# Float32 numerator, normalisation on GpSimd, and a keys-values product with exp(k) stationary, in a three-stage kernel

## The chip, the cores and the metric

The kernel runs on one core of one Trainium2 chip as a single launch. The metric is the time of one execution on the device, in microseconds; each version is run several times and the median is given. Before the change the median of 3 runs is 1889.26 us (1889.13 to 1890.09).

## What is computed

Three stages follow one another. The first is a linear attention with exponential features; its result is the input of a dense layer, whose result is the input of a routed one.

```python
def phi(x):
    proj = einsum('bhsd,df->bhsf', x, w_phi)              # 8 batches, 8 heads, 576 tokens, 64 -> 128
    proj = proj - max(abs(proj), axis=-1, keepdims=True)
    return concatenate([exp(proj), exp(-proj)], axis=-1)  # 256 features
q_p, k_p = phi(q), phi(k)
kv  = einsum('bhsf,bhsd->bhfd', k_p, v)
z   = sum(k_p, axis=2)
num = einsum('bhsf,bhfd->bhsd', q_p, kv)
den = einsum('bhsf,bhf->bhs', q_p, z) + 1e-06
x   = num / den                                           # -> 4608 tokens of 512
h   = x @ w_in;  x = (h * cos(h)) @ w_out                 # 512 -> 2048 -> 512
# then each token goes to one of 8 experts (argmax of its logits), 512 -> 1024 -> 512
```

## The kernel before, in words

The attention works through 16 items, each of two batches (`bb`) and two heads (`h`). An item's 576 tokens are cut into five groups of blocks, `PR`; a group has two blocks of 128 columns, the middle one has one, with the leftover 64 tokens of both batches. The routine `step(j,s)` writes ten steps per item: keys, values and queries of item j, and the products with kv of item j-1. Within a step TensorE's instructions are written first; the work of the other engines stands in the lists `now`, `nxt` and `nxt2` and is written in the same step, the next one, or the one after that. The framework's scheduler then orders each engine's instructions, and every engine runs its own in that order.

For each group, by engine:

- TensorE projects keys and queries, three float32r products each (lines 130 to 132), into banks `pj`. VectorE takes the largest absolute value (line 137) and subtracts it (line 138), which gives `t_k` and `t_q`.
- ScalarE takes both exponentials of `t_k` (lines 149, 150) into `ke`. TensorE multiplies v, extended by a column of ones, with `ke` (line 168): v's 65 columns are the stationary operand, 256 columns of `ke` stream. The operands are float32, and each product stands as two instruction pairs (a weight load and a matmul) in the trace.
- When a batch is through, ScalarE copies its sums out (line 171), TensorE transposes them in four pieces (line 180), and VectorE writes kv, and z repeated 64 times, as a high part (lines 185, 186) and a remainder (lines 187, 188), both float32r.
- TensorE transposes `t_q` (line 203), ScalarE takes both exponentials into `qe` (lines 213, 214). A high part `qh` is copied, by VectorE or in one of five groups by ScalarE (line 219), and GpSimd subtracts it to get the remainder `ql` (line 220).
- `num` (line 241) makes numerator and denominator of half a batch (`u`): six float32r products of 288 columns per head. ScalarE takes ln, negation and exp (lines 249 to 251). VectorE multiplies (line 254), GpSimd prepares a Newton step (line 255), and VectorE applies it (line 257). After an item's last half SyncE's queue writes the result `xo` to the device's memory (line 260).

The last 20 of the 170 attention steps share the engines with the dense layer's start. There `stage` fetches a chunk of the dense weights through SyncE's queue (lines 411, 413), `decode` turns float64 bits into two float32r parts (ScalarE lines 427 and 433, VectorE lines 428 to 431, GpSimd line 434), 32 times in all, and the dense layer's first products (line 463) begin; VectorE has two instructions for each of their activations (lines 478, 481).

Of the kernel before, what the change touches and what calls it, by code (L numbers as in the profile page):

```python
# [43 lines left out]
def attention(tc, ctx, cpool, S, ps, ident, q, k, v, w_phi, xt):  # L44
    """generator; writes xt [4,128,4608], columns in the order of `chunk`"""
# [107 lines left out]
    kvp={}; kvt={}; kvsb={}  # L153
    def kv(i,g):
        """accumulate (v|1)^T k_p"""
# [3 lines left out]
        for idx in range(2*n):  # L159
            h,cc=chunk(c0,idx//2,idx%2)  # L160
            parts=[(0,0,P)] if cc<4 else ([(1,0,P)] if cc>4 else [(0,0,64),(1,64,P)])
            for (bb,p0,p1) in parts:
# [5 lines left out]
                nc.tensor.matmul(o,vh[p0:p1,h,cc,:],e[p0:p1,idx*256:(idx+1)*256],start=first and h==0,stop=last,skip_group_check=True)  # L168
                if last and h==1:
                    kt=S("kvt",f"kvt_{i}_{bb}")[0:D+1,:]  # L170
                    now.append(lambda kt=kt,p=kvp[i,bb]: nc.scalar.copy(kt,p[0:D+1,:]))
                    kvt[i,bb]=kt

    def kvfin(i,bb):
        """kv|z with f on partitions, z repeated 64 times; head 0: [kv|z], head 1: [z|kv]"""
        if i<0: return
        kt=kvt.pop((i,bb))
        pt=ps.tile([P,512],F32,tag="tr",name=f"pkv_{i}_{bb}")
        for g in range(4):
            nc.tensor.transpose(pt[:,g*(D+1):(g+1)*(D+1)],kt[:,g*P:(g+1)*P],ident[0:D+1,0:D+1])  # L180
        hi,lo=(S(x,f"{x}_{i}_{bb}",F32R).rearrange("p (s g d) -> p s g d",s=2,d=D) for x in ("kvh","kvl"))
        pv=pt[:,:4*(D+1)].rearrange("p (h s d) -> p s h d",h=2,s=2)
        z=pv[:,:,:,D:D+1].to_broadcast([P,2,2,D])
        def vec():
# [1 line left out]
            nc.vector.tensor_copy(hi[:,:,1:3,:],z)
            nc.vector.tensor_tensor(lo[:,:,0::3,:],pv[:,:,:,0:D],f32(hi[:,:,0::3,:]),ALU.subtract)
            nc.vector.tensor_tensor(lo[:,:,1:3,:],z,f32(hi[:,:,1:3,:]),ALU.subtract)
# [4 lines left out]
    def qtile(i,bb):
        if (i,bb) not in qq:
            qq[i,bb]=(ap.tile([P,2,2,576],F32R,tag="qh",name=f"qh_{i}_{bb}",bufs=3),
                      ap.tile([P,2,2,576],F32R,tag="ql",name=f"ql_{i}_{bb}",bufs=3))
        return qq[i,bb]
    def qexp(i,g,tt):
        """transpose proj - max, exp, split"""
# [12 lines left out]
        def vec():  # L212
            nc.scalar.activation(e[:,:,0,:w],pv,AF.Exp,scale=1.0)
            nc.scalar.activation(e[:,:,1,:w],pv,AF.Exp,scale=-1.0)
        def vec2():
            for (bb,s0,s1,d0) in parts:
                qh,ql=qtile(i,bb)
                sl=slice(d0,d0+s1-s0)
                (nc.scalar.copy if g==3 else nc.vector.tensor_copy)(qh[:,:,:,sl].rearrange("p h s c -> p (h s) c"),e[:,:,:,s0:s1].rearrange("p h s c -> p (h s) c"))  # L219
                nc.gpsimd.tensor_tensor(ql[:,:,:,sl],e[:,:,:,s0:s1],f32(qh[:,:,:,sl]),ALU.subtract)  # L220
        now.append(vec); nxt.append(vec2)

    xos={}
    def num(i,bb,u):
# [8 lines left out]
        rr=ap.tile([P,288],F32,tag="rr",name=f"rr_{i}_{bb}_{u}")
        pns=[]
        for h in range(2):
            pn=ps.tile([P,512],F32,tag="nm",name=f"pn_{i}_{bb}_{u}_{h}")[:,0:288]
            nmm=0
            for s in range(2):
                w=slice(h*P,(h+1)*P)
                for (A,B) in ((hi,qh),(hi,ql),(lo,qh)):  # L240
                    nc.tensor.matmul(pn,A[:,s,w],B[:,h,s,su],start=nmm==0,stop=nmm==5)
# [4 lines left out]
        # 1/den: exp(-ln den), then a Newton step  # L246
        def vec():
            for pn,a,b in pns:
                nc.scalar.activation(rr[a,:],pn[b,:],AF.Ln,bias=eps[b,:],scale=1.0)
# [700 lines left out]
```

## Time and profile before

| quantity | value |
|---|---|
| median of 3 runs | 1889.26 us |
| span of the profiled execution, first to last instruction | 1886.5 us |
| busy share of the span, TensorE matmul / VectorE / ScalarE / GpSimd | 93% / 65% / 54% / 36% |
| issues of the 16 results `xo` (line 260), first and last | 62.9 us, 524.3 us |
| last VectorE instruction of the last `decode` (line 431) | 621.0 us |

The page gives no time of its own for the profiled execution besides its span; the median is 2.8 us above that, for what lies around the instructions. In the views a row names the source line, the engine, the operation, the tile written and the tiles read, and the shapes. PE is TensorE's matmuls, PEld its weight loads, DVE VectorE, ACT ScalarE, POOL GpSimd, SP SyncE. A matmul's recorded time includes the time until its result has arrived, so matmuls that follow closely overlap in the records; their pace is the distance from start to start.

### The profile page before, as it was taken

To read this page: it belongs to the slowest core of one execution; us is meant where nothing else is said; L and a number is where in the kernel's file an instruction comes from. 1 tells how busy PE (TensorE), PEld (TensorE's weight loads), DVE (VectorE), ACT (ScalarE), POOL (GpSimd) and SP (SyncE) were. 2 spreads that over 40 slices of the span, in tenths; PEclk is the share of its full clock that TensorE was granted. 3 is DMA by queue.
4 is the path that set the end of the run, shared out by engine and by line. 5 is a ranking of instruction groups with operands and counts; after the bars stand their busy time and mean duration, and the time that the engine had idled before them with its cause. 6 is when DMAs were issued, how large, how long until landed. Compare 5 with 4: busy or idle time off the path is not lost. (4 is left out here: it accounts for less than half of the span.)

```text
span 1886.5 us, 27617 instructions
## 1 busy us (share of the span) xinstructions
PE 1759.9 (93%) x9782; PEld 1470.0 (78%) x9782; DVE 1232.9 (65%) x2168; ACT 1016.7 (54%) x1862; POOL 686.4 (36%) x556
## 2 busy tenths in 40 slices
PE   7989889898778899999999999999988999999996
PEld 6777777776556688888888888888877999999975
DVE  7999999999899545453545454444466655555555
ACT  5787877877655333334343433343345555555555
POOL 3454444545555424243424343333222211111121
PEclk9999999999899899999999999999998999999998
DMA  6223232231343010101010101010136865767766
GB/s 170 73 80 94 61 99 72 81 90 55 108 142 122 0 46 1 45 1 46 1 45 1 45 0 45 1 45 3 36 124 249 294 224 201 257 226 226 224 221 223
DMA packets 143448, 192.27 MB, mean 102 GB/s; under 512 B 64831, under 2 KB 89535, under 8 KB 143298
## 3 DMA queue, kind: packets, MB, share of 16 engines
q1 hardware_dynamic: 135346, 168.82, 27.9%
q0 software_dynamic: 7952, 21.54, 3.4%
...
## 5 line engine op out<-in xcount | busy, mean ns | idle before, releaser
L463 PE MATMUL ph<-x,w 128*128 128x512 f32 x1728 | 435.6, 401 | 32.8 <-DVE fr L481 23.2
L463 PEld LDWEIGHTS ph<-x,w 128*128 128x128 f32 x1728 | 325.9, 192 | 113.7 <-DVE fr L481 29.1
L493 PE MATMUL acc<-gh,w 128*128 128x512 f32 x1152 | 358.6, 392 | 2.9 <-DVE gh L483 1.7
L484 POOL TENSOR_TENSOR gl<-fr,gh 128x512 fp32r<-128x512 f32 x144 | 190.1, 1321 | 364.4 <-DVE gh L483 296.0
L672 DVE TENSOR_TENSOR m<-raw,m 128x512 fp32r<-128x512 f32 x336 | 219.4, 693 | 134.9 <-ACT m L671 134.6
L493 PEld LDWEIGHTS acc<-gh,w 128*128 128x128 f32 x1152 | 217.9, 189 | 48.8 <-DVE gh L483 2.0
L220 POOL TENSOR_TENSOR ql<-qe,qh 128x1024 fp32r<-128x1024 f32 (+1 forms) x96 | 175.5, 1835 | 176.9 <-DVE qh L219 147.1
L671 ACT CAST m<-raw 128x512 fp32r<-128x512 f32 x336 | 195.7, 618 | 71.2 <-PE mh L712 31.4
L493 PE MATMUL acc<-gl,w 128*128 128x512 f32 x576 | 225.7, 392 | 3.3 <-POOL gl L484 3.3
L476 ACT ACTIVATE n<-ph 128x512 int32<-128x512 f32 x144 | 85.6, 595 | 255.1 <-PE ph L463 252.1
L478 DVE SCALAR_TENSOR_TENSOR fr<-ph,n 128x512 f32<-128x512 f32 x144 | 99.2, 689 | 181.8 <-ACT n L476 177.9
L712 PEld LDWEIGHTS mh<-xT,m 128*128 128x128 f32 x1728 | 210.8, 192 | 2.4 <-DVE hl L715 0.5
L712 PE MATMUL mh<-xT,m 128*128 128x256 f32 x1728 | 211.4, 283 | 0.2 <-DVE hl L715 0.2
L481 DVE SCALAR_TENSOR_TENSOR fr<-fr,ph 128x512 f32<-128x512 f32 x144 | 98.7, 686 | 159.0 <-ACT fr L480 159.0
L724 PE MATMUL po<-m,hh 128*128 128x512 f32 x576 | 181.6, 396 | 0.0
L479 ACT ACTIVATE fr<-fr 128x512 f32<-128x512 f32 x144 | 91.1, 632 | 145.1 <-DVE fr L478 143.8
L168 PE MATMUL kv<-ke,v 128*65 128x256 f32 (+1 forms) x640 | 148.9, 383 | 1.1 <-ACT ke L150 0.9
...
L493 PEld LDWEIGHTS acc<-gl,w 128*128 128x128 f32 x576 | 109.1, 189 | 27.2 <-POOL gl L484 4.4
L724 PEld LDWEIGHTS po<-m,hh 128*128 128x128 f32 x576 | 106.3, 190 | 20.4
L724 PE MATMUL po<-m,hl 128*128 128x512 f32 x288 | 113.1, 393 | 0.0
L168 PEld LDWEIGHTS kv<-ke,v 128*65 128x65 f32 (+1 forms) x640 | 74.6, 137 | 29.6 <-issue 3.4
(212 smaller groups left out, 3178.6 us busy)
## 6 DMA issues: line engine op xcount, KB each, us to landing
raw<-in_moe_w_dram SPq DMA_DIRECT2D x179, 512.0 KB, 6.4
...
```

The costliest lines, as they stand in the source:

```text
L168: nc.tensor.matmul(o,vh[p0:p1,h,cc,:],e[p0:p1,idx*256:(idx+1)*256],start=first and h==0,stop=last,skip_group_check=True)
L220: nc.gpsimd.tensor_tensor(ql[:,:,:,sl],e[:,:,:,s0:s1],f32(qh[:,:,:,sl]),ALU.subtract)
L463: nc.tensor.matmul(ph,A[:,ws],xhl[u,d][k],start=n[0]==0,stop=n[0]==11); n[0]+=1
L478: nc.vector.scalar_tensor_tensor(g,ph,INV2PI,n,op0=ALU.mult,op1=ALU.subtract)
L479: nc.scalar.activation(g,g,AF.Sin,scale=math.pi)
L481: nc.vector.scalar_tensor_tensor(g,g,-0.5,ph,op0=ALU.add,op1=ALU.mult)
L484: nc.gpsimd.tensor_tensor(gl,g,f32(gh),ALU.subtract)
L493: nc.tensor.matmul(accs[u][d],A[:,ws],B,start=(f==0 and k==0),stop=(f==NF-1 and k==2))
L671: nc.scalar.copy(h,a)
L672: nc.vector.tensor_tensor(l,a,f32(h),ALU.subtract)
L712: nc.tensor.matmul(ph[:,f2*T:(f2+1)*T],A[:,ws],B[d//2][:,xs],start=n==0,stop=n==11); n+=1
L724: nc.tensor.matmul(po[c],A[:,ws],B,start=(f==0 and j==0),stop=(f==NF2-1 and j==2))
```

## The change

Four things change in the attention; nothing changes behind it.

- kv: 128 columns of `ke` are stationary now and the 65 columns of v with ones stream. The sums come out with features on partitions, so the copy (line 171) and the transposes (line 180) go; VectorE copies kv and z from the bank into one float32 tile `kvz`.
- `qexp` writes the exponentials into one float32 tile `qx`, in place of `qe`, `qh` and `ql`.
- `num` has two float32 products per head and half, in place of six float32r ones.
- Per half, ScalarE writes the negated denominator and VectorE copies the numerator to `xo`. Per batch, ScalarE makes one ln and one exp over 576 columns, and GpSimd makes four instructions over 576 columns: the Newton step and the multiplication into `xo`.

```diff
                 if first and h==0:
                     kvp[i,bb]=ps.tile([P,512],F32,tag="kv",name=f"kv_{i}_{bb}")
-                o=kvp[i,bb][0:D+1,h*256:(h+1)*256]
-                nc.tensor.matmul(o,vh[p0:p1,h,cc,:],e[p0:p1,idx*256:(idx+1)*256],start=first and h==0,stop=last,skip_group_check=True)
-                if last and h==1:
-                    kt=S("kvt",f"kvt_{i}_{bb}")[0:D+1,:]
-                    now.append(lambda kt=kt,p=kvp[i,bb]: nc.scalar.copy(kt,p[0:D+1,:]))
-                    kvt[i,bb]=kt
+                for s in range(2):
+                    o=kvp[i,bb][:,(2*h+s)*66:(2*h+s)*66+D+1]
+                    nc.tensor.matmul(o,e[p0:p1,idx*256+s*F:idx*256+(s+1)*F],vh[p0:p1,h,cc,:],start=first and h==0 and s==0,stop=last,skip_group_check=True)
...
     def kvfin(i,bb):
...
-        for g in range(4):
-            nc.tensor.transpose(pt[:,g*(D+1):(g+1)*(D+1)],kt[:,g*P:(g+1)*P],ident[0:D+1,0:D+1])
...
         def vec():
-            nc.vector.tensor_copy(hi[:,:,0::3,:],pv[:,:,:,0:D])
-            nc.vector.tensor_copy(hi[:,:,1:3,:],z)
-            nc.vector.tensor_tensor(lo[:,:,0::3,:],pv[:,:,:,0:D],f32(hi[:,:,0::3,:]),ALU.subtract)
-            nc.vector.tensor_tensor(lo[:,:,1:3,:],z,f32(hi[:,:,1:3,:]),ALU.subtract)
+            nc.vector.tensor_copy(kz[:,:,0::3,:],pv[:,:,:,0:D])
+            nc.vector.tensor_copy(kz[:,:,1:3,:],z)
...
     def qexp(i,g,tt):
...
         def vec():
-            nc.scalar.activation(e[:,:,0,:w],pv,AF.Exp,scale=1.0)
-            nc.scalar.activation(e[:,:,1,:w],pv,AF.Exp,scale=-1.0)
-        def vec2():
             for (bb,s0,s1,d0) in parts:
-                qh,ql=qtile(i,bb)
-                sl=slice(d0,d0+s1-s0)
-                (nc.scalar.copy if g==3 else nc.vector.tensor_copy)(qh[:,:,:,sl].rearrange("p h s c -> p (h s) c"),e[:,:,:,s0:s1].rearrange("p h s c -> p (h s) c"))
-                nc.gpsimd.tensor_tensor(ql[:,:,:,sl],e[:,:,:,s0:s1],f32(qh[:,:,:,sl]),ALU.subtract)
-        now.append(vec); nxt.append(vec2)
+                qx=qtile(i,bb)
+                for k,sign in ((0,1.0),(1,-1.0)):
+                    nc.scalar.activation(qx[:,:,k,d0:d0+s1-s0],pv[:,:,s0:s1],AF.Exp,scale=sign)
+        now.append(vec)
...
     def num(i,bb,u):
...
             for s in range(2):
-                w=slice(h*P,(h+1)*P)
-                for (A,B) in ((hi,qh),(hi,ql),(lo,qh)):
-                    nc.tensor.matmul(pn,A[:,s,w],B[:,h,s,su],start=nmm==0,stop=nmm==5)
-                    nmm+=1
+                nc.tensor.matmul(pn,kz[:,s,h*P:(h+1)*P],qx[:,h,s,su],start=s==0,stop=s==1)
...
         def vec():
             for pn,a,b in pns:
-                nc.scalar.activation(rr[a,:],pn[b,:],AF.Ln,bias=eps[b,:],scale=1.0)
-                nc.scalar.activation(dn[a,:],pn[b,:],AF.Identity,bias=neps[b,:],scale=-1.0)
+                nc.scalar.activation(dn[a,su],pn[b,:],AF.Identity,bias=neps[b,:],scale=-1.0)
+                nc.vector.tensor_copy(xo[a,sl],pn[a,:])
+        now.append(vec)
+        if u==0: return
...
+        def inv():
+            nc.scalar.activation(rr,dn,AF.Ln,scale=-1.0)
             nc.scalar.activation(rr,rr,AF.Exp,scale=-1.0)
-        def vec2():
-            for pn,a,b in pns:
-                nc.vector.tensor_tensor(xo[a,sl],pn[a,:],rr[a,:],ALU.mult)
+        def mul():
             nc.gpsimd.tensor_tensor(dn,dn,rr,ALU.mult)
-        def vec3():
-            nc.vector.scalar_tensor_tensor(xo[:,sl],dn,2.0,xo[:,sl],op0=ALU.add,op1=ALU.mult)
-            if (bb,u)==(1,1):
+            nc.gpsimd.tensor_scalar(dn,dn,2.0,None,op0=ALU.add)
+            nc.gpsimd.tensor_tensor(dn,dn,rr,ALU.mult)
+            nc.gpsimd.tensor_tensor(xs,xs,dn,ALU.mult)
+            if bb==1:
                 bp,hp=items[i]
                 nc.sync.dma_start(xt[hp,:,bp*1152:(bp+1)*1152],xo)
-        now.append(vec); nxt.append(vec2); nxt2.append(vec3)
+        nxt.append(inv); nxt2.append(mul)
```

The scheduler's order at three places follows, before and after. Names carry the group, batch, half or head; the last number of a name tells buffers apart; "x4" is four such instructions in a row.

On TensorE, in the middle of the attention, the end of the second half's numerator of batch 0 (`pn_0_1_1`: batch, half, head) before the change:

```order
L241 MATMUL pn_0_1_1_3295<-qh_0_2858,kvh_0_3144 128x288
L241 MATMUL pn_0_1_1_3295<-ql_0_2859,kvh_0_3144 128x288
L241 MATMUL pn_0_1_1_3295<-qh_0_2858,kvl_0_3145 128x288
L180 MATMUL pkv_1_3302<-ident,kvt_1_3257 128x65 x4
L168 MATMUL kv_0_3330<-ke_0_3243,v_2780 65x256 x2
L203 MATMUL ptt_2_3309<-ident,t_q_2_3273 128x128 x4
```

The same place on TensorE after the change, the whole half with both heads:

```order
L223 MATMUL pn_0_1_0_2831<-qx_0_2469,kvz_0_2703 128x288 x2
L223 MATMUL pn_0_1_1_2834<-qx_0_2469,kvz_0_2703 128x288 x2
L168 MATMUL kv_0_2855<-v_2398,ke_0_2792 128x65 x4
L193 MATMUL ptt_2_2839<-ident,t_q_2_2824 128x128 x4
L168 MATMUL kv_0_2855<-v_2398,ke_0_2792 128x65 x4
```

The half has four products in place of twelve, the transposes of kv are gone, and a group's kv has eight products of 65 columns in place of four of 256.

On VectorE, the same stretch of an item before the change (`t_q_2` is what the transposes `ptt_2` read):

```order
L257 SCALAR_TENSOR_TENSOR xo_3218<-dn_0_0_3219,xo_3218 128x288
L138 TENSOR_TENSOR t_q_2_3273<-pj_q_2_3266,m_q_2_3283 128x512
L185 CAST kvh_1_3307<-pkv_1_3302 128x2x2x64
L186 CAST kvh_1_3307<-pkv_1_3302 128x2x128
L187 TENSOR_TENSOR kvl_1_3308<-pkv_1_3302,kvh_1_3307 128x2x2x64
L188 TENSOR_TENSOR kvl_1_3308<-pkv_1_3302,kvh_1_3307 128x2x128
L254 TENSOR_TENSOR xo_3218<-pn_0_1_0_3288,rr_0_1_3287 64x288
L254 TENSOR_TENSOR xo_3218<-pn_0_1_1_3295,rr_0_1_3287 64x288
L219 CAST qh_0_3241<-qe_2_3314 128x4x256
L137 TENSOR_REDUCE m_k_4_3357<-pj_k_4_3335 128x2
```

And on VectorE after the change:

```order
L178 COPY kvz_1_2838<-kv_1_2665 128x2x2x64
L179 COPY kvz_1_2838<-kv_1_2665 128x2x128
L136 TENSOR_REDUCE m_k_2_2825<-pj_k_2_2809 128x4
L136 TENSOR_REDUCE m_q_2_2828<-pj_q_2_2817 128x4
L137 TENSOR_TENSOR t_k_2_2816<-pj_k_2_2809,m_k_2_2825 128x512
L137 TENSOR_TENSOR t_q_2_2824<-pj_q_2_2817,m_q_2_2828 128x512
L230 COPY xo_2778<-pn_0_1_0_2831 64x288
L230 COPY xo_2778<-pn_0_1_1_2834 64x288
L136 TENSOR_REDUCE m_k_4_2883<-pj_k_4_2864 128x2
```

Nothing stands between the subtractions `t_k_2` and `t_q_2` and the reductions ahead of them; the copies to `xo` read banks alone and wait for no `rr`.

On SyncE's queue, where the attention ends, before the change (`st_0`, `st_1` are chunks of w_in and w_out, `xr` the dense layer's next input):

```order
L411 DMA st_0_6367<-in_moe_w_in_dram 128x4x256
L413 DMA st_1_6427<-in_moe_w_out_dram 128x1024
L260 DMA xt<-xo_6234 128x1152
L413 DMA st_1_6498<-in_moe_w_out_dram 128x1024
L443 DMA xr_0_7072<-xt 128x512
```

And after the change:

```order
L397 DMA st_0_5409<-in_moe_w_in_dram 128x4x256
L399 DMA st_1_5461<-in_moe_w_out_dram 128x1024
L246 DMA xt<-xo_5306 128x1152
L399 DMA st_1_5518<-in_moe_w_out_dram 128x1024
L429 DMA xr_0_6094<-xt 128x512
```

The order of the queue is the same; the write of `xo` follows GpSimd's multiplication now, where it followed VectorE's line 257.

More of the change, by code (lines that the diff above doesn't have):

```diff
@@ L59, in attention @@
     nc.scalar.preload_act_table_set("natural_log_exp_and_others")
-    eps=cpool.tile([P,1],F32,name="eps"); nc.vector.memset(eps,1e-6)
     neps=cpool.tile([P,1],F32,name="neps"); nc.vector.memset(neps,-1e-6)
@@ L151, in kexp @@
         es[i,g]=e
-    kvp={}; kvt={}; kvsb={}
+    kvp={}; kvsb={}
     def kv(i,g):
@@ L166, in kv @@
                     kvp[i,bb]=ps.tile([P,512],F32,tag="kv",name=f"kv_{i}_{bb}")
-                o=kvp[i,bb][0:D+1,h*256:(h+1)*256]
-                nc.tensor.matmul(o,vh[p0:p1,h,cc,:],e[p0:p1,idx*256:(idx+1)*256],start=first and h==0,stop=last,skip_group_check=True)
-                if last and h==1:
-                    kt=S("kvt",f"kvt_{i}_{bb}")[0:D+1,:]
-                    now.append(lambda kt=kt,p=kvp[i,bb]: nc.scalar.copy(kt,p[0:D+1,:]))
-                    kvt[i,bb]=kt
+                for s in range(2):
+                    o=kvp[i,bb][:,(2*h+s)*66:(2*h+s)*66+D+1]
+                    nc.tensor.matmul(o,e[p0:p1,idx*256+s*F:idx*256+(s+1)*F],vh[p0:p1,h,cc,:],start=first and h==0 and s==0,stop=last,skip_group_check=True)
     def kvfin(i,bb):
         if i<0: return
-        kt=kvt.pop((i,bb))
-        pt=ps.tile([P,512],F32,tag="tr",name=f"pkv_{i}_{bb}")
-        for g in range(4):
-            nc.tensor.transpose(pt[:,g*(D+1):(g+1)*(D+1)],kt[:,g*P:(g+1)*P],ident[0:D+1,0:D+1])
-        hi,lo=(S(x,f"{x}_{i}_{bb}",F32R).rearrange("p (s g d) -> p s g d",s=2,d=D) for x in ("kvh","kvl"))
-        pv=pt[:,:4*(D+1)].rearrange("p (h s d) -> p s h d",h=2,s=2)
+        pt=kvp.pop((i,bb))
+        kz=S("kvh",f"kvz_{i}_{bb}").rearrange("p (s g d) -> p s g d",s=2,d=D)
+        pv=pt[:,:4*66].rearrange("p (h s d) -> p s h d",h=2,s=2)
         z=pv[:,:,:,D:D+1].to_broadcast([P,2,2,D])
         def vec():
-            nc.vector.tensor_copy(hi[:,:,0::3,:],pv[:,:,:,0:D])
-            nc.vector.tensor_copy(hi[:,:,1:3,:],z)
-            nc.vector.tensor_tensor(lo[:,:,0::3,:],pv[:,:,:,0:D],f32(hi[:,:,0::3,:]),ALU.subtract)
-            nc.vector.tensor_tensor(lo[:,:,1:3,:],z,f32(hi[:,:,1:3,:]),ALU.subtract)
+            nc.vector.tensor_copy(kz[:,:,0::3,:],pv[:,:,:,0:D])
+            nc.vector.tensor_copy(kz[:,:,1:3,:],z)
         now.append(vec)
-        kvsb[i,bb]=(hi.rearrange("p s g d -> p s (g d)"),lo.rearrange("p s g d -> p s (g d)"))
+        kvsb[i,bb]=kz.rearrange("p s g d -> p s (g d)")
     qq={}
@@ L194, in qtile @@
         if (i,bb) not in qq:
-            qq[i,bb]=(ap.tile([P,2,2,576],F32R,tag="qh",name=f"qh_{i}_{bb}",bufs=3),
-                      ap.tile([P,2,2,576],F32R,tag="ql",name=f"ql_{i}_{bb}",bufs=3))
+            qq[i,bb]=ap.tile([P,2,2,576],F32,tag="qx",name=f"qx_{i}_{bb}",bufs=3)
         return qq[i,bb]
@@ L226, in num @@
         if i not in xos: xos[i]=ap.tile([P,9*P],F32,tag="xo",name=f"xo_{i}")
-        xo=xos[i]
-        hi,lo=kvsb[i,bb]
-        qh,ql=qtile(i,bb)
+        if u==0: dns[i,bb]=ap.tile([P,576],F32,tag="dn",name=f"dn_{i}_{bb}")
+        xo=xos[i]; dn=dns[i,bb]
+        kz=kvsb[i,bb]
+        qx=qtile(i,bb)
         sl=slice(bb*576+u*288,bb*576+(u+1)*288)
         su=slice(u*288,(u+1)*288)
-        dn=ap.tile([P,288],F32,tag="dn",name=f"dn_{i}_{bb}_{u}")
-        rr=ap.tile([P,288],F32,tag="rr",name=f"rr_{i}_{bb}_{u}")
         pns=[]
```

6 lines of the change are left out of this document (3 added, 3 removed).

## The prediction

> **What bounds the kernel now.** I read the page first, for where each engine is full. Its slices are 47 us each.
>
> ```profile
> span 1886.5 us, 27617 instructions
> ...
> PE   7989889898778899999999999999988999999996
> ...
> DVE  7999999999899545453545454444466655555555
> ```
>
> The attention fills the first eleven slices, and there VectorE is at nine tenths or more while TensorE has eights and sevens. From slice 14 on TensorE is full and VectorE half idle. The busy times by stage:
>
> ```profile
> core 0: us, PE busy (x) PEld busy (x) DVE busy (x) ACT busy (x) POOL busy (x), PEclk, DMA share, GB/s
> 100.00:454.00 354.00, 318.97 (x2233) 264.22 (x2232) 325.30 (x613) 279.79 (x590) 170.62 (x132) 1.00 0.28 80
> 454.00:525.00 71.00, 50.38 (x248) 39.86 (x248) 65.47 (x105) 51.36 (x91) 37.30 (x28) 0.88 0.25 83
> 525.00:621.00 96.00, 73.55 (x280) 55.24 (x280) 95.45 (x131) 48.46 (x84) 55.71 (x37) 0.91 0.39 127
> 640.00:700.00 60.00, 60.00 (x288) 48.78 (x288) 24.71 (x53) 22.77 (x37) 18.12 (x15) 1.00 0.11 36
> ```
>
> The groups of instructions from 100 to 454 us, VectorE's that the change touches:
>
> ```profile
> L257 DVE SCALAR_TENSOR_TENSOR xo<-dn,xo 128x288 f32<-128x288 f32 x48 | 54.0, 1126 | 0.0
> L254 DVE TENSOR_TENSOR xo<-pn,rr 64x288 f32<-64x288 f32 x97 | 44.0, 454 | 19.2 <-ACT rr L251 17.7
> L219 DVE CAST qh<-qe 128x1024 fp32r<-128x1024 f32 x36 | 24.8, 688 | 0.8
> L186 DVE CAST kvh<-pkv 128x256 fp32r<-128x256 f32 x24 | 9.8, 407 | 0.0
> L188 DVE TENSOR_TENSOR kvl<-pkv,kvh 128x256 fp32r<-128x256 f32 x24 | 9.8, 407 | 0.0
> L187 DVE TENSOR_TENSOR kvl<-pkv,kvh 128x256 fp32r<-128x256 f32 x24 | 9.8, 407 | 0.0
> L219 DVE CAST qh<-qe 128x256 fp32r<-128x256 f32 x24 | 5.8, 285 | 0.0
> ```
>
> Line 257 runs four times per item, so its 48 runs are 12 items in 354 us: 29.5 us per item. Of these VectorE is busy 27.1 (325.30/12) and idle mostly for `rr`; TensorE is busy 26.6 (318.97/12). From 454 to 621 us VectorE is at 92%, then 99%: decoding, the last items and the dense layer's start share it. After 640 us TensorE decides, in a part that the change leaves alone. So VectorE sets both the items' pace and the length of the passage, with TensorE close behind in the items; the question is what TensorE's new products cost. Its waits among the same groups:
>
> ```profile
> L203 PE MATMUL ptt<-ident,t_q 128*128 128x128 f32 x216 | 34.4, 277 | 26.8 <-DVE t_q L138 19.6 <-DVE kT_lo L119 7.3
> L241 PE MATMUL pn<-qh,kvh 128*128 128x288 f32 x192 | 60.4, 316 | 5.2 <-DVE kvh L186 2.9 <-DVE xo L254 2.3
> ```
>
> 32.0 us in 12 items, 2.7 per item, all for VectorE.
>
> **TensorE's products, per item.** Their pace is read from starts in the timeline, at a place without waits:
>
> ```profile
> 302.04 0.30 PE L241 MATMUL pn<-ql,kvh 128*128 128x288 f32 x1
> 302.17 0.29 PE L241 MATMUL pn<-qh,kvl 128*128 128x288 f32 x1
> 302.30 1.46 PE L168 MATMUL kv<-ke,v 128*65 128x256 f32 x6
> ...
> 304.07 0.28 PE L131 MATMUL pj_k<-wph_hi,kT_lo 128*128 128x256 f32 x1
> 304.18 0.28 PE L132 MATMUL pj_k<-wph_lo,kT_hi 128*128 128x256 f32 x1
> 304.30 0.60 PE L203 MATMUL ptt<-ident,t_q 128*128 128x128 f32 x4
> ```
>
> And, later, the transposes of kv, then the weight loads that belong to the six matmuls at 302.30:
>
> ```profile
> 308.35 0.41 PE L180 MATMUL pkv<-ident,kvt 65*128 65x65 f32 x4
> ```
>
> ```profile
> 302.18 1.13 PEld L168 LDWEIGHTS kv<-ke,v 128*65 128x65 f32 x6
> ```
>
> One float32r matmul of 288 columns takes 0.13 us, one of 256 takes 0.115, one float32 pass of 256 columns (1.46-0.38)/5 = 0.216 (0.38 being the record of one), a transpose of 128 columns (0.60-0.27)/3 = 0.11, one of kv's (0.41-0.22)/3 = 0.062. Per item there are 20 kv products with two passes, 48 numerator products, 54 projections, 36 transposes and 8 of kv: 40 x 0.216 + 48 x 0.13 + 54 x 0.115 + 36 x 0.11 + 8 x 0.062 = 8.6 + 6.2 + 6.2 + 4.0 + 0.5 = 25.5 us. With the waits of 2.7 that is 28.2; the last 1.3 us go to weight loads and pipeline ends around each wait.
>
> After it, the numerator has 16 float32 products, so 32 passes of 288 columns: 0.216 x 288/256 = 0.243 each, 7.8 us (+1.6). kv has 40 products, 80 passes, each a load of 128 columns and a stream of 65. The stream is short, 0.216 x 65/256 = 0.055 us, so the load sets the pace, and no row shows a true float32 load of 128 columns outside transposes. From below, kv's transposes load 128 columns in 0.062; from above stands a load's whole record, 0.19:
>
> ```profile
> L241 PEld LDWEIGHTS pn<-ql,kvh 128*128 128x128 f32 x192 | 36.2, 188 | 0.0
> L168 PEld LDWEIGHTS kv<-ke,v 128*65 128x65 f32 x384 | 49.9, 137 | 17.0
> ```
>
> I take 0.115, the projections' pace, in which a load of 128 columns fits: 63 more columns cost 51 ns of record whether the small load is float32 or the large one float32r, so the type does not seem to matter. That is 80 x 0.115 = 9.2 us (+0.6; ends 5.0 and 15.2). The transposes go (-0.5). TensorE: 25.5 + 1.6 + 0.6 - 0.5 = 27.2 us.
>
> This needs a load to run beside the previous matmul. The six loads start at 302.18 and spread over 1.13 us, while the six matmuls start at 302.30 and follow at 0.216, the pace of their streams alone; so they do. The Trainium skill, "TensorE: Matmul & The Clock Gate", Part 3, "The mechanism", says that a weight load overlaps matmuls in flight only when it goes to another row group; these all use the same rows, so this trace disagrees. By that rule the load, about P/1.2 or 107 ns by the same page's "LDWEIGHTS", would be added to the stream, and kv would take an estimated 13 us.
>
> **The other engines, per item.** VectorE loses lines 254 (44.0/12 = 3.7 us), 257 (4.5), 219 (30.6/12 = 2.5), 187 and 188 (1.6), 12.3 in all, and gains 8 copies of 64x288 from banks, between line 186's 0.41 for 256 and line 254's 0.45: 3.5 us. 27.1 - 8.8 = 18.3 us. ScalarE and GpSimd:
>
> ```profile
> L220 POOL TENSOR_TENSOR ql<-qe,qh 128x1024 fp32r<-128x1024 f32 x48 | 114.1, 2378 | 116.3 <-DVE qh L219 94.5 <-ACT qh L219 21.7
> L249 ACT ACTIVATE rr<-pn,eps 64x288 f32<-64x288 f32 x96 | 47.7, 497 | 12.0 <-PE pn L241 10.2
> L255 POOL TENSOR_TENSOR dn<-dn,rr 128x288 f32<-128x288 f32 x49 | 39.4, 803 | 55.4 <-ACT qT_hi L118 28.1 <-ACT rr L251 27.3
> L251 ACT ACTIVATE rr<-rr 128x288 f32<-128x288 f32 x48 | 21.1, 440 | 0.9
> L171 ACT COPY kvt<-kv 65x512 f32<-65x512 f32 x24 | 13.9, 581 | 0.0
> L219 ACT CAST qh<-qe 128x1024 fp32r<-128x1024 f32 x12 | 12.6, 1046 | 0.4
> ```
>
> ScalarE loses 95.3/12 = 7.9 us and gains four runs over 576 columns at 0.68 (between 0.44 for 288 and 1.05 for 1024) and two small exponentials: 23.3 to some 18.5. GpSimd loses lines 220 and 255, over 12.8 us (153.5/12), and gains eight runs over 576 columns; by line 255's 0.80 for 288 they take 1.6 each, 13 us. A scalar addition on GpSimd has no row; between 0.8 and 3 us it leaves GpSimd at 11 to 16 of 28 us, so it is covered, and would decide only at ten times that.
>
> New waits: the copies of `kvz` hold a kv bank until VectorE has read it, but two banks alternate, and the next use of one is almost an item later. GpSimd's four runs follow ScalarE's exp in a chain of about 6 us; behind it on GpSimd stands only the next batch's chain, and `xo` has two buffers.
>
> With VectorE at 18 and ScalarE at 19 of some 28 us, TensorE becomes the bound. In the scheduled order, after the last product of `pj_q` TensorE has a numerator (8 passes, 1.9 us) and half of a group's kv (0.9) before `ptt` needs `t_q`, against 0.3 of pipeline and three VectorE runs of 0.7 (2.4 us): covered by 0.4 us. I add 0.6 us for ends and short waits, 27.8 us per item. From the end of the first slice, in which inputs are still awaited, to 454 us there are (454 - 47)/29.5 = 14 items: 14 x 1.7 = 24 us. The ends are 27.2 (32 us) and 29.0, with nearly all waits still there (7 us).
>
> **The passage, 454 to 621 us.** VectorE's removed groups there (458 to 525 us):
>
> ```profile
> L257 DVE SCALAR_TENSOR_TENSOR xo<-dn,xo 128x288 f32<-128x288 f32 x8 | 9.4, 1174 | 0.1
> ...
> L254 DVE TENSOR_TENSOR xo<-pn,rr 64x288 f32<-64x288 f32 x14 | 6.3, 451 | 2.2 <-ACT rr L251 2.0
> ```
>
> With the last items' runs of lines 187, 188 and 219 (three of each, by the rows above 0.41, 0.41 and up to 0.69, 4.5 us) 20 us go, and 14 copies at 0.44 come (6.2). Records overlap a little; I count 12 us, all on the bound. Against it, the last write of `xo` now waits for GpSimd's chain, which stands between the dense layer's own subtractions there, and the chunk of w_out behind it on SyncE's queue lands later; a decode that waits for that chunk holds all of VectorE. GpSimd needs some 8 us more than line 257 did, and I find about as much VectorE work ahead of that decode: 2 us lost, between 0 and 9. Net 10 us, between 3 and 16.
>
> **Sum.** 24 + 10 = 34 us of the profiled 1886.5, so a span of 1852.5; with the 2.8 us between span and median, 1855 us.
>
> **The rivals.** *Slower, as weight loads are not hidden:* a pass of kv costs a load plus its stream, 0.115 + 0.055 = 0.17 us. kv takes 13.6 us, TensorE 31.6 + 0.6 = 32.2, 2.7 more than now; 14 x 2.7 - 10 = +28, 1917 us (0.19 gives 1939). It decides from 0.145 us per pass on, where item and passage cancel. For it: a short stream leaves less to hide a load behind than any float32 product shows. Against: the loads at 302.18. The overlap rule of the Trainium skill, on the page named above, ends here too, at an estimated 1908.
>
> *TensorE bound with its old waits:* queues in order keep 2 us of waits per item, though for other engines: 29.0 per item, 7 + 10 us, 1872. For it: ScalarE and VectorE stay two thirds full, and `ptt` has only 0.4 us of cover. Against: all 2.7 us of now are for an engine that loses a third of its work.
>
> *Much faster:* float32 loads go at the transposes' 0.062, TensorE needs 23.0, and with 2 us of waits items take 25: 14 x 4.5 + 10 = 73 us, 1816. Against: the 65-column loads of line 168 fit the slower pace.
>
> **How the numbers follow.** I give the forecast 0.64, old waits 0.20, unhidden loads 0.10, fast loads 0.06. A measurement of this kernel tells 0.2%, 3.8 us, from no change. Faster is 0.64 + 0.06 and old waits but for the 0.03 in which the passage gives its gain back too: 0.87; same 0.03; slower 0.10. Range: from 32 + 16 = 48 us (1841) less some for rounding, 1838, to 7 + 3 = 10 us (1879), taken as 1880; this leaves out the unhidden and the fast loads.
>
> **What would show it.** Right: issues of `xo` 27.8 us apart; kv passes at 0.115 us, numerator passes at 0.243; VectorE near two thirds busy in the items and TensorE's waits for `t_q` below 1 us per item; VectorE still full in the passage, which ends some 34 us earlier. Wrong: kv passes over 0.145, items over 29 us with waits of TensorE for ScalarE or VectorE, or VectorE waiting in the passage for a decode's input behind the last `xo` write.

## The result and the profile after

The changed kernel takes 1848.16 us (median of 4 runs, 1846.29 to 1849.99) against 1889.20 (4 runs, 1888.77 to 1890.09): a ratio of 0.9781, 95% interval 0.9767 to 0.9795. The forecast was 1855, from 1838 to 1880. The profiled execution's own time is 1849.99, the longest of the four, and its span 1848.3; the span before is 1886.5. So 38.2 us of span went.

The page after the change: span, and the busy tenths in 40 slices of 46 us.

```profile
span 1848.3 us, 27492 instructions
...
PE   8999999997787999999999999999898999999996
...
DVE  6777777779997454544444544454556555655555
```

In the attention (slices 1 to 9) the two engines have changed places: TensorE has nines from the second slice on, VectorE sevens. Slices 10 to 12, the passage, are as before: VectorE nines, TensorE sevens and eights. Busy time by stage:

```profile
core 0: us, PE busy (x) PEld busy (x) DVE busy (x) ACT busy (x) POOL busy (x), PEclk, DMA share, GB/s
47.00:400.00 353.00, 352.72 (x2644) 322.93 (x2643) 256.53 (x501) 250.26 (x524) 156.81 (x119) 1.00 0.31 88
...
495.00:580.00 85.00, 63.79 (x256) 48.36 (x255) 84.52 (x117) 43.16 (x74) 49.04 (x33) 0.96 0.35 108
```

TensorE is busy in 99.9% of the items' stretch, VectorE in 73%, ScalarE in 71%, GpSimd in 44%. From 100 to 400 us the list of waits for TensorE has no row at all; before it had 2.7 us per item. From 495 to 580 us VectorE is still at 99%.

The groups of the changed lines from 100 to 400 us, and two rows of the timeline that give the pace of the passes:

```profile
L168 PE MATMUL kv<-v,ke 128*128 128x65 f32 (+1 forms) x896 | 107.1, 272 | 0.0
...
L223 PE MATMUL pn<-qx,kvz 128*128 128x288 f32 x352 | 92.5, 406 | 0.0
...
L230 DVE COPY xo<-pn 64x288 f32<-64x288 f32 x90 | 40.7, 452 | 44.3 <-ACT dn L229 43.4
L241 POOL TENSOR_SCALAR dn<-dn 128x576 f32<-128x576 f32 x23 | 38.0, 1652 | 2.0
...
L240 POOL TENSOR_TENSOR dn<-dn,rr 128x576 f32<-128x576 f32 x23 | 32.4, 1408 | 140.9 <-ACT rr L238 140.9
```

```profile
302.77 2.10 PE L223 MATMUL pn<-qx,kvz 128*128 128x288 f32 x8
304.70 1.00 PE L168 MATMUL kv<-v,ke 128*128 128x65 f32 x8
```

The next product starts 1.93 us after the first of eight numerator passes (304.70 - 302.77): 0.241 each, as forecast (0.243). Inside a run of kv passes the median from start to start is 0.112 (forecast 0.115). A float32 addition of a number on GpSimd, which had no row before, takes 1.65 us, a product of 576 columns 1.41.

All kernels can be laid beside each other by when `xo` of an item is written, when the first decode starts and the last ends, when the dense layer's first result leaves its bank (`x1T`), and the end (us from the span's start; e1 to e8 are the experiments below). The last rows sum the records of the decode's four lines on VectorE, and give VectorE's busy time between the write of item 13 and the first `x1T`:

```
                 before  after    e1      e2      e3      e4      e5      e6      e7      e8
xo of item 0       62.9   61.9    63.9    62.4    58.5    65.0    66.9    61.3    61.7    61.6
xo of item 13     446.5  412.5   422.9   429.9   406.7   413.1   422.1   411.9   412.3   412.5
xo of item 15     524.3  483.9   494.4   505.4   475.6   493.8   491.9   469.8   480.3   477.5
first decode      459.9  418.6   431.0   442.0   416.1   422.4   428.5   417.9   418.3   419.5
last decode ends  621.7  579.3   588.5   602.8   575.9   587.3   586.0   567.3   577.2   577.8
first x1T         637.5  597.8   607.3   618.2   588.9   604.5   604.8   584.5   594.4   590.2
end              1886.5 1848.3  1856.5  1867.1  1836.7  1856.9  1853.8  1832.0  1844.6  1841.9
decode lines, sum 106.6  115.8   108.7   105.6   101.6   116.6   109.1   106.5   114.9   101.5
VectorE, 13-x1T   175.4  169.6   170.1   174.5   163.2   180.8   167.7   159.6   168.3   159.8
```

Read by columns: the kernel after is 1.0 us ahead at item 0, 34.0 at item 13 (13 intervals of 27.0 us instead of 29.5), 39.8 at the first `x1T`, 38.2 at the end. So the items gave more than forecast, the passage less, and the rest a loss of 1.6. The last two rows are the ones that explain the passage; the second counts all of VectorE's work, as in e1 and e5 the decode's lines are shorter and the casts `gh<-fr` longer by 6.0 us in 18 runs.

### The profile page after: what moved, and what is told of

It reads as the page before. It is cut to its first block, busy times and chain, and to the rows that moved or that the text cites. A ratio compares the mean times of both kernels' runs of the same rounds, so it can differ in the third digit from the quotient of the medians.

```text
span 1848.3 us, 27492 instructions
## 1 busy us (share of the span) xinstructions
PE 1762.9 (95%) x10038; PEld 1509.3 (82%) x10038; DVE 1121.5 (61%) x1959; ACT 947.1 (51%) x1715; POOL 647.6 (35%) x524
## 3 DMA queue, kind: packets, MB, share of 16 engines
q8 instruction: 85, 1.39, 0.3%
## 5 line engine op out<-in xcount | busy, mean ns | idle before, releaser
L449 PEld LDWEIGHTS ph<-x,w 128*128 128x128 f32 x1728 | 325.5, 191 | 110.5 <-DVE fr L467 27.8
L168 PEld LDWEIGHTS kv<-v,ke 128*128 128x128 f32 (+1 forms) x1280 | 148.4, 191 | 13.3 <-issue 7.1
L168 PE MATMUL kv<-v,ke 128*128 128x65 f32 (+1 forms) x1280 | 154.0, 272 | 1.9 <-ACT ke L148 1.8
L223 PE MATMUL pn<-qx,kvz 128*128 128x288 f32 x512 | 138.3, 413 | 9.6 <-DVE xo L230 9.6
L479 PEld LDWEIGHTS acc<-gl,w 128*128 128x128 f32 x576 | 109.1, 189 | 27.8 <-POOL gl L470 4.9
L710 PEld LDWEIGHTS po<-m,hh 128*128 128x128 f32 x576 | 106.0, 189 | 20.2
L223 PEld LDWEIGHTS pn<-qx,kvz 128*128 128x128 f32 x512 | 93.8, 193 | 31.8 <-DVE xo L230 10.9
```

The source lines that it names most:

```text
L168: nc.tensor.matmul(o,e[p0:p1,idx*256+s*F:idx*256+(s+1)*F],vh[p0:p1,h,cc,:],start=first and h==0 and s==0,stop=last,skip_group_check=True)
L223: nc.tensor.matmul(pn,kz[:,s,h*P:(h+1)*P],qx[:,h,s,su],start=s==0,stop=s==1)
L449: nc.tensor.matmul(ph,A[:,ws],xhl[u,d][k],start=n[0]==0,stop=n[0]==11); n[0]+=1
L479: nc.tensor.matmul(accs[u][d],A[:,ws],B,start=(f==0 and k==0),stop=(f==NF-1 and k==2))
L710: nc.tensor.matmul(po[c],A[:,ws],B,start=(f==0 and j==0),stop=(f==NF2-1 and j==2))
```

## The experiments

Each ratio is to the kernel before, measured beside the experiment (medians 1888.0 to 1888.8 us).

**e1, the old product of keys and values in the changed kernel.**

```diff
-    o=kvp[i,bb][:,(2*h+s)*66:(2*h+s)*66+D+1]
-    nc.tensor.matmul(o,e[p0:p1,idx*256+s*F:idx*256+(s+1)*F],vh[p0:p1,h,cc,:],...)
+    o=kvp[i,bb][0:D+1,h*256:(h+1)*256]
+    nc.tensor.matmul(o,vh[p0:p1,h,cc,:],e[p0:p1,idx*256:(idx+1)*256],...)
...
+    now.append(lambda kt=kt,p=kvp[i,bb]: nc.scalar.copy(kt,p[0:D+1,:]))
...
+    nc.tensor.transpose(pt[:,g*(D+1):(g+1)*(D+1)],kt[:,g*P:(g+1)*P],ident[0:D+1,0:D+1])
```

Expected: 

> The changed kernel with the keys-values product as it was (v stationary, copy by ScalarE, four transposes), all else changed. If the gain is VectorE's relief and kv is neutral on TensorE (40 x 0.216 + 8 x 0.062 = 9.1 us against 80 x 0.112 = 9.0 us per item), items take 27.0 to 27.6 us and the time is 1848 to 1858. If the new kv itself, without copy and transposes, carries the gain, most of it goes: items over 28.5 us, over 1870.

Measured: 1859.49 us, ratio to before 0.9848 [0.9831, 0.9864], 1.5 us beyond the first range. Items take 27.6 us instead of 27.0. TensorE is busy in all of 100 to 400 us in both kernels, with no row of waits, so the 0.6 us are its own work. Summed from start to start over ten items, the old kv takes 7.79 us per item, its transposes 0.59, the new kv 8.33. These sums hide a part of kv, as the rows behind a group of kv show, in e1 and then in the kernel after:

```profile
307.04 1.89 PE L167 MATMUL kv<-ke,v 128*65 128x256 f32 x8
308.58 0.47 PE L129 MATMUL pj_k<-wph_hi,kT_hi 128*128 128x256 f32 x1
308.89 0.28 PE L130 MATMUL pj_k<-wph_hi,kT_lo 128*128 128x256 f32 x1
```

```profile
305.98 1.00 PE L168 MATMUL kv<-v,ke 128*128 128x65 f32 x8
306.80 0.37 PE L129 MATMUL pj_k<-wph_hi,kT_hi 128*128 128x256 f32 x1
307.00 0.29 PE L130 MATMUL pj_k<-wph_hi,kT_lo 128*128 128x256 f32 x1
```

In e1 eight passes at 0.216 us last to 308.77, but the projection behind them is recorded from 308.58, and its successor follows only after 0.31 us. If such a first projection is counted at its pace of 0.115 and the rest given to kv, the old kv takes 8.7 us per item and the new one 8.8: as products the two cost the same, and the 0.6 us are nearly all the transposes. In this kernel, where TensorE sets the pace, the new kv is worth some 11 us (8.2 by the spans) because the transposes are gone.

**e2, the new product of keys and values alone**, the rest as before.

Its edit is the reverse of e1's, made to the kernel before. Expected: 

> The kernel before with the keys-values product alone changed. VectorE's work stays as it was (the four runs that write kv and z in two parts remain), so if VectorE sets the pace items stay at 29.2 to 29.6 us and the time within 6 us of 1889. If the copy and the transposes were on the path, items fall by 1 us or more, to 1875 or less.

Measured: 1870.98 us, 0.9910 [0.9893, 0.9927], 18 us under the kernel before: the second expectation held, not the first. Items take 28.3 us, and VectorE, busy in 94% of 100 to 400 us, still sets their pace. Where VectorE's 1.2 us per item went shows in its groups; first the kernel before, then e2, both from 100 to 400 us:

```profile
L257 DVE SCALAR_TENSOR_TENSOR xo<-dn,xo 128x288 f32<-128x288 f32 x41 | 47.1, 1150 | 0.0
L254 DVE TENSOR_TENSOR xo<-pn,rr 64x288 f32<-64x288 f32 x82 | 37.2, 454 | 16.0 <-ACT rr L251 14.8
```

```profile
L251 DVE SCALAR_TENSOR_TENSOR xo<-dn,xo 128x288 f32<-128x288 f32 x43 | 42.7, 993 | 0.0
L248 DVE TENSOR_TENSOR xo<-pn,rr 64x288 f32<-64x288 f32 x86 | 38.8, 451 | 7.2 <-ACT rr L245 6.1
```

The refinement, the same instruction on the same shape, is 157 ns shorter (0.6 us in four runs), and the wait for `rr` falls from 16.0/41 = 0.39 to 7.2/43 = 0.17 us per run (0.9 in four; two other waits grow, so that VectorE's idle time as a whole falls from 2.4 to 1.8 us per item). So the copy and the transposes had been on the path, though VectorE sets the pace. That an instruction has two lengths was the first hint of what bounds the passage; e3 shows where they come from.

**e3, the old normalisation** with the new products.

```diff
-    nc.scalar.activation(dn[a,su],pn[b,:],AF.Identity,bias=neps[b,:],scale=-1.0)
-    nc.vector.tensor_copy(xo[a,sl],pn[a,:])
...
+    nc.scalar.activation(rr[a,:],pn[b,:],AF.Ln,bias=eps[b,:],scale=1.0)
+    nc.scalar.activation(dn[a,:],pn[b,:],AF.Identity,bias=neps[b,:],scale=-1.0)
...
+    nc.vector.tensor_tensor(xo[a,sl],pn[a,:],rr[a,:],ALU.mult)
+    nc.gpsimd.tensor_tensor(dn,dn,rr,ALU.mult)
...
+    nc.vector.scalar_tensor_tensor(xo[:,sl],dn,2.0,xo[:,sl],op0=ALU.add,op1=ALU.mult)
```

Expected: 

> The changed kernel with the normalisation as it was (per half: ScalarE ln, negation, exp; VectorE multiplication and last Newton step; GpSimd one product). VectorE gets about 4.7 us per item back and stands at some 23 of 27 us. If TensorE's passes alone set the pace, items stay at 27.0 to 27.5 us, and the time is 1843 to 1856. If moving the normalisation to GpSimd was needed, VectorE's queue holds TensorE again: items 28 us or more, 1862 or more.

Measured: 1837.84 us, 0.9732 [0.9716, 0.9749], 10 us faster than the change as made and under both expected ranges. Items take 26.8 us, still at TensorE's pace, so the work that was moved off VectorE was not worth moving there. VectorE's group of the refinement, from 100 to 400 us:

```profile
L239 DVE SCALAR_TENSOR_TENSOR xo<-dn,xo 128x288 f32<-128x288 f32 x45 | 20.2, 448 | 0.0
```

448 ns, where the kernel before had 1150. Beside it GpSimd no longer runs `ql`, 2.4 us at a time. The trace of before agrees by itself: of its 64 refinements (line 257) 16 ran with GpSimd idle, at 0.446 us on average, and 46 for most of their length beside a product or difference on GpSimd, at 1.39.

**e4, the numerator split in six float32r products again**, the normalisation on GpSimd (one buffer less for `rr`).

```diff
-    nc.tensor.matmul(pn,kz[:,s,h*P:(h+1)*P],qx[:,h,s,su],start=s==0,stop=s==1)
+    for (A,B) in ((hi,qh),(hi,ql),(lo,qh)):
+        nc.tensor.matmul(pn,A[:,s,w],B[:,h,s,su],start=nmm==0,stop=nmm==5)
...
+    nc.gpsimd.tensor_tensor(ql[:,:,:,sl],e[:,:,:,s0:s1],f32(qh[:,:,:,sl]),ALU.subtract)
```

Expected: 

> The changed kernel with the numerator as before: operands in two float32r parts (VectorE's copies, GpSimd's subtractions, two more VectorE runs per kv) and six products; the new kv and the normalisation on GpSimd stay. One of the two buffers of the reciprocals is given up for room. TensorE: 27.0 - 7.8 + 6.3 = 25.5 us per item. VectorE rises to about 23, GpSimd to about 24. If TensorE alone decides, items take 25.5 to 26.2 us and the time falls to 1826 to 1838, under the changed kernel. If GpSimd's queue, at 24 of 25.5 us, comes on the path or slows VectorE, items take 27 us or more, and the time is 1850 or more.

Measured: 1858.65 us, 0.9842 [0.9828, 0.9855]. The second expectation held in its time. The six products take 7.01 us per item against 7.74, and items 26.6 us: three engines are then nearly full, and TensorE waits again.

```profile
100.00:400.00 300.00, 288.04 (x2464) 280.67 (x2464) 267.47 (x533) 225.14 (x442) 260.20 (x168) 1.00 0.32 89
```

```profile
PE pj_k L129 <- DVE t_k L137: 11.1, 11, 1.1
```

One us per item is lost to VectorE, item 13 is written no earlier than in the kernel after, and 10 us go on the way to item 15. The cheaper split and GpSimd's normalisation do not go together in this kernel; what the missing buffer of `rr` has in this was not separated.

**e5, a stream of 128 columns instead of 65 in the kv passes**; the 63 columns more are read but not used.

```diff
-    o=kvp[i,bb][:,(2*h+s)*66:(2*h+s)*66+D+1]
-    ...,vh[p0:p1,h,cc,:],...
+    o=kvp[i,bb][:,(2*h+s)*128:(2*h+s+1)*128]
+    ...,vh[p0:p1,(9*h+cc)*(D+1):(9*h+cc)*(D+1)+128],...
```

Expected: 

> The changed kernel with 128 columns streamed in each kv pass in place of 65; the 63 added columns are the next chunk's and are not used. If the weight load sets the pace of a kv pass (0.112 us) and the stream runs beside the next load, a stream of 128 columns (about 0.107 us at 0.216 for 256) still fits under it: passes stay near 0.112 to 0.115, items at 27.0 us, the time within 4 us of the changed kernel's 1848. If load and stream add up in part, each of 80 passes per item grows by up to 0.053 us: items 31 us, some 1900 us or more.

Measured: 1857.33 us, 0.9838 [0.9822, 0.9855], 9 us more than the change, beyond the 4 expected. A part of it is no product: the loads of v stand later in SyncE's queue at the start (the first at 9.1 us instead of 7.1, the fourth at 13.2 instead of 9.1), and TensorE waits for one,

```profile
PE kv L170 <- DMA v<-in_v_dram: 4.1, 1, 4.1
```

and item 0 is written 5.0 us later. The added memset itself takes 0.14 us; why the loads were ordered so isn't known. Items take 0.35 us more (27.32). Streams one after the other with their loads would have added 80 x 63 columns, 4.2 us per item. Inside a run of kv passes the median from start to start stays 0.112; only the second pass of a run follows its first later (0.111 us instead of 0.059), which is 0.3 of the 0.35 us. So inside a run the stream doesn't set the pace and hides beside what does, by all signs the load of 128 columns. The overlap rule of the Trainium skill, "TensorE: Matmul & The Clock Gate", Part 3, "The mechanism" (a weight load overlaps with matmuls in flight only when its row group differs), does not hold for these passes. The same section also lets a load that goes to the background weight buffer run ahead, and with that the passes agree.

**e6, no Newton step in items 14 and 15.** Three of GpSimd's four instructions are left out there, 12 in all, so those two items keep the unrefined reciprocal.

```diff
-    nc.gpsimd.tensor_tensor(dn,dn,rr,ALU.mult)
-    nc.gpsimd.tensor_scalar(dn,dn,2.0,None,op0=ALU.add)
-    nc.gpsimd.tensor_tensor(dn,dn,rr,ALU.mult)
-    nc.gpsimd.tensor_tensor(xs,xs,dn,ALU.mult)
+    if i<14:
+        ...
+    nc.gpsimd.tensor_tensor(xs,xs,dn if i<14 else rr,ALU.mult)
```

Expected: 

> The changed kernel without the Newton step for the last two of the 16 items: 12 of their 16 GpSimd instructions are left out, and the reciprocals there are exp(-ln) alone. In the passage the four VectorE lines of the decode take 115.9 us against 106.5 before the change. If that is GpSimd's longer chains running at the same time, the four lines fall by some 7 us and the time by 5 to 9 us. If the last write of xo, which waits for GpSimd, is what costs, the write comes some 6 us earlier and VectorE's idle time in the passage falls by 2 to 4 us with the lines' sum unchanged. If neither, the time stays within 2 us of the changed kernel's.

Measured: 1837.96 us (1834.21 to 1841.78), 0.9739 [0.9726, 0.9752]. 12 instructions of GpSimd, 19 us of its time, are worth 10 us of the kernel, somewhat more than the first expectation, though the items before are the same (412.5 and 411.9). From the write of item 13 to the first `x1T`, in the kernel after and in e6:

```profile
412.50:597.80 185.30, 143.60 (x627) 112.61 (x625) 169.64 (x231) 98.04 (x169) 107.84 (x73) 0.90 0.32 102
411.90:584.50 172.60, 138.34 (x625) 107.64 (x625) 159.63 (x231) 97.64 (x168) 87.53 (x60) 0.95 0.34 110
```

Of the 12.7 us by which this stretch is shorter, 10.0 are VectorE's: the same 231 instructions keep it busy for 159.63 us instead of 169.64. Its idle time falls by the other 2.7; whether that comes from the write of item 15, which is 14.1 us earlier, or from TensorE's granted clock, 0.95 instead of 0.90 here, isn't shown. How GpSimd's instructions lengthen VectorE's shows in the timelines of the kernel after, VectorE's first and then GpSimd's:

```profile
464.67 0.41 DVE L414 TENSOR_SCALAR d_t<-d_t 128x512 f32<-128x512 f32 x1
465.12 1.39 DVE L415 TENSOR_SCALAR d_t<-d_t 128x512 int32<-128x512 int32 x1
...
468.90 0.42 DVE L415 TENSOR_SCALAR d_t<-d_t 128x512 int32<-128x512 int32 x1
...
476.01 0.93 DVE L230 COPY xo<-pn 64x288 f32<-64x288 f32 x2
...
479.19 1.76 DVE L416 SCALAR_TENSOR_TENSOR d_t<-st,d_t 128x512 int32<-128x512 int32 x1
480.98 1.64 DVE L417 SCALAR_TENSOR_TENSOR d_t<-st,d_t 128x512 int32<-128x512 int32 x1
```

```profile
464.83 1.39 POOL L470 TENSOR_TENSOR gl<-fr,gh 128x512 fp32r<-128x512 f32 x1 [0.36 <-DVE gh L469]
...
475.50 1.75 POOL L420 TENSOR_TENSOR w<-d_t,w 128x512 fp32r<-128x512 f32 x1
...
478.95 1.45 POOL L242 TENSOR_TENSOR dn<-dn,rr 128x576 f32<-128x576 f32 x1
480.36 1.71 POOL L420 TENSOR_TENSOR w<-d_t,w 128x512 fp32r<-128x512 f32 x1
```

The same shift on VectorE (line 415) takes 0.42 us at 468.90, with GpSimd idle, and 1.39 at 465.12: there it begins 0.3 us after a subtraction on GpSimd and ends 0.3 after its end. The steps with two inputs in SBUF stretch as well (1.76 and 1.64 instead of 0.68). The two copies from a bank at 476.01 do not, 0.93 for both beside 1.75 of GpSimd; nor do the steps `fr` with two inputs of 128x512, one of them a bank (0.69 beside GpSimd and without). Over all decodes of the kernel after, 18 of the one-input steps ran with GpSimd idle, at 0.415 us on average, and 36 for most of their length beside a product or difference on GpSimd, at 1.24. The Trainium skill, "SBUF — State Buffer", "Who interferes with whom", has the mechanism: VectorE and GpSimd share a pair of SBUF ports, which one instruction holds to its end; `tensor_scalar` in its fast form and any instruction with two SBUF inputs want it, one with at most one input in SBUF and outside that form doesn't. These rows agree.

**e7, the same 12 instructions, written in the program behind the write of `xo`**, so that no result depends on them; items 14 and 15 again use the unrefined reciprocal.

```diff
+    if i<14: newton()
+    nc.gpsimd.tensor_tensor(xs,xs,dn if i<14 else rr,ALU.mult)
     if bb==1:
         ...
         nc.sync.dma_start(xt[hp,:,bp*1152:(bp+1)*1152],xo)
+    if i>=14: newton()
```

Expected: 

> The kernel after, but in items 14 and 15 the product of xo and its write go ahead of the three Newton instructions, which GpSimd still runs, on the same tiles, for nobody: xo is multiplied by the unrefined reciprocal there. GpSimd has the same 16 instructions in the passage as the kernel after; only nobody waits for 12 of them. Theory (GpSimd's instructions slow VectorE's decodes while both run): the four decode lines still sum to 112 to 118 us (after 115.8, without the 12 instructions 106.5), and the end stays within 4 us of the kernel after, 1844 to 1852. Rival (the last write waits for the chain, and what is queued behind it comes late): the write of item 15 comes some 10 us earlier, and the end follows it, to 1836 to 1840.

Measured: 1846.77 us (1844.02 to 1848.12), 0.9774 [0.9759, 0.9789]. The decode's four lines on VectorE from 400 to 625 us, in the kernel after, in e6 and in e7:

```profile
L416 DVE SCALAR_TENSOR_TENSOR d_t<-st,d_t 128x512 int32<-128x512 int32 x32 | 29.9, 936 | 0.4
L414 DVE TENSOR_SCALAR d_t<-d_t 128x512 f32<-128x512 f32 x32 | 29.2, 916 | 0.0
L415 DVE TENSOR_SCALAR d_t<-d_t 128x512 int32<-128x512 int32 x32 | 28.9, 905 | 0.4
L417 DVE SCALAR_TENSOR_TENSOR d_t<-st,d_t 128x512 int32<-128x512 int32 x32 | 27.5, 862 | 0.2
```

```profile
L416 DVE TENSOR_SCALAR d_t<-d_t 128x512 int32<-128x512 int32 x32 | 27.5, 863 | 0.4
L415 DVE TENSOR_SCALAR d_t<-d_t 128x512 f32<-128x512 f32 x32 | 27.3, 857 | 0.0
L417 DVE SCALAR_TENSOR_TENSOR d_t<-st,d_t 128x512 int32<-128x512 int32 x32 | 27.0, 848 | 0.4
L418 DVE SCALAR_TENSOR_TENSOR d_t<-st,d_t 128x512 int32<-128x512 int32 x32 | 24.2, 759 | 0.2
```

```profile
L417 DVE TENSOR_SCALAR d_t<-d_t 128x512 f32<-128x512 f32 x32 | 31.5, 988 | 0.0
L419 DVE SCALAR_TENSOR_TENSOR d_t<-st,d_t 128x512 int32<-128x512 int32 x32 | 28.5, 896 | 0.4
L418 DVE TENSOR_SCALAR d_t<-d_t 128x512 int32<-128x512 int32 x32 | 28.0, 879 | 0.4
L420 DVE SCALAR_TENSOR_TENSOR d_t<-st,d_t 128x512 int32<-128x512 int32 x32 | 26.5, 830 | 0.2
```

115.5, 106.0 and 114.5 us (busy time, in which records that overlap count once) for the same 128 instructions on the engine that is full there. With the 12 instructions run for nothing, the time is that of the change. But the write of item 15 came only 3.6 us earlier, not 10: the scheduler put two of the last three Newton instructions ahead of the product (line 245) in GpSimd's order.

```profile
473.93 1.89 POOL L240 TENSOR_TENSOR dn<-dn,rr 128x576 f32<-128x576 f32 x1 [1.17 <-ACT rr L238]
477.04 1.83 POOL L241 TENSOR_SCALAR dn<-dn 128x576 f32<-128x576 f32 x1
478.84 1.39 POOL L245 TENSOR_TENSOR xo<-xo,rr 128x576 f32<-128x576 f32 x1
```

So e7 by itself does not refute the rival of the late write, whose forecast was an end that follows the write: it came 3.7 us earlier by the spans, 1.4 by the medians, within their scatter. What speaks against that rival is VectorE's account: it is busy for 168.3 us from item 13 to the first `x1T`, nearly as in the change, and the list of its waits from 412 to 598 us in the kernel after has no row for a decode's input. A late write could act through idle time alone, and that is the smaller part of what e6 gained.

**e8, the old normalisation in items 14 and 15 alone**, nothing left out.

```diff
     def num(i,bb,u):
         if i<0: return
+        if i>=14: return num_old(i,bb,u)
```

Expected: 

> The kernel after with the old normalisation (VectorE's products, one product on GpSimd) in items 14 and 15 alone. The old normalisation everywhere gave 1837.8: its item 13 was written 5.8 us earlier than in the kernel after, its end came 11.6 us earlier. Theory (half of that is the passage, where less GpSimd work runs beside the decodes): item 13 is written as in the kernel after, at 412 to 413 us, the decode lines sum to 101 to 106 us instead of 115.8, and the end comes 4 to 8 us before that of the kernel after, 1840 to 1844. Rival (VectorE's own 20 us of work come back into the passage and eat the gain): 1846 to 1852.

Measured: 1844.33 us (1842.94 to 1846.13), 0.9765 [0.9750, 0.9780]; span 1841.9, 6.4 below the change's. Item 13 is written at 412.5 as in the change, the decode lines sum to 101.5. VectorE has eight refinements back in the passage, and products in place of copies, and is still busy for 9.8 us less up to the first `x1T` (159.8 against 169.6); 2.2 us of that are lost to more idle time. The median is 3.8 us below the change's, just outside what was expected (1840 to 1844), with intervals that overlap; together with e3 and e6 it points the same way.

**e9, reciprocals on VectorE**, eight per item, nothing on GpSimd; 1e-6 isn't added to the denominator.

```diff
+    nc.vector.reciprocal(rr[a,:],pn[b,:])
...
+    nc.vector.tensor_tensor(xo[a,sl],pn[a,:],rr[a,:],ALU.mult)
```

Expected: 

> The new products, and a normalisation on VectorE alone: eight reciprocals of 64x288 from the bank and eight products per item; no logarithm, exponential or Newton step, nothing on GpSimd (1e-6 isn't added to the denominator). Beside the old normalisation with the new products (1837.8) VectorE loses four runs of 1.13 us per item and gains eight reciprocals. If one takes 0.4 to 0.5 us, as a copy of that shape, VectorE stays at some 21 of 26.8 us, TensorE sets the pace of the items, and the passage loses ScalarE's and GpSimd's work: 1832 to 1838. Rival (a reciprocal is an iterated operation): from 1.3 us each VectorE sets the pace again, and at 2 us items take 33 us: above 1900.

Measured: 2000.04 us, 1.0585 [1.0571, 1.0599]. VectorE's group from 100 to 400 us:

```profile
L229 DVE RECIPROCAL rr<-pn 64x288 f32<-64x288 f32 x65 | 127.1, 1955 | 12.0 <-PE pn L223 10.3
```

1.96 us, over four times a copy of the shape; VectorE sets the pace at some 37 us per item. The rival had it, though with 33 us. The best kernel found is e3.

## Why the prediction was right, and where its terms were off

The mechanism of the items was right: TensorE takes over, its float32 passes run at the forecast pace, and VectorE's removed work pays for them. Term by term:

- **Waits** (forecast 2.7 us per item gone, 0.6 left for ends and short waits): no wait of TensorE is left from 100 to 400 us, so the rival of old waits has nothing to stand on. Little of the 0.6 is found: the transposes take 0.2 us more than their pace gives, and the projections 6.2, as their pace gives, if the rest of the kv pass ahead of them is given to kv (as shown at e1).
- **Numerator** (forecast 7.8 us per item): 7.74 by the pace of 0.242.
- **kv** (forecast 80 x 0.115 = 9.2): 8.33 from start to start, 8.8 with what the projections' records hide. This and the allowance above are the mis-sized terms. The forecast counts every pass alike, at a pace that is a little too slow (0.112 measured): the second pass of a run starts 0.059 us after the first, the length of its stream, and 16 of the 80 passes have 64 rows, of which some start 13 ns after the pass of the other half. The two terms together make the difference between 27.8 and 27.0 us per item, some 11 us over 14 items.
- **Items** (forecast 24 us): 34.0 by item 13, of which 1.0 is there at item 0. e5 shows the fear behind the slowest rival, a load and a stream one after the other, to be unfounded.
- **VectorE** (forecast 18.3 us per item): 256.53/353 x 27.0 = 19.6. The forecast took whole records off a busy time in which records overlap (305 us of them in the 276 busy us from 100 to 400 us before). It cost nothing, as TensorE set the pace. More telling is line 257, taken off at 1126 ns: by e3, and by its own runs with GpSimd idle, only some 447 of them are its own work; the rest came from GpSimd's instructions beside it. Of the room on VectorE a good part came from the work that GpSimd lost.
- **Passage** (forecast 12 us of VectorE's work less, 2 lost, net 10): 39.8 - 34.0 = 5.8 by the first `x1T`. Behind that 1.6 are lost again; the time from there to the end is 1247.5 to 1252.5 us over the ten kernels of the table, whose work there is the same, and 1.6 lie well within that. The step that failed is "I count 12 us, all on the bound": it counts VectorE's instructions at their old lengths. VectorE's busy time between item 13 and the first `x1T` fell by 5.8 us (175.4 to 169.6), and that is the whole gain. The decode's 128 instructions grew by 9.2 us in the kernel after (106.6 to 115.8), since GpSimd's chain runs beside them; with the chain gone (e6) they are at 106.5, and the lead at the first `x1T` is 53.0, 18.4 more than at item 13 (in an execution 3.8 us under e6's median). The late chunk of w_out, which the prediction charged with 2 us, shows in no wait of VectorE.

That the total came so near is in part luck: +10 us in the items met -4 in the passage and -1.6 behind it. 2.7 us more are the forecast's allowance between span and median, since the profiled execution after was the slowest of its four. The prediction looked at GpSimd as a queue, with 16 of 28 us at most and "covered"; it did not ask what GpSimd's running does to the engine beside it. Line 257 at 1126 ns, against 454 for line 254 on the same 288 columns, was a hint in the trace of before. Two readings of its page were loose, though nothing was worked out from them: in the attention TensorE has nines too, in four of eleven slices, and VectorE's first and eleventh slices are a seven and an eight.
